# Weights loaded at once, magnitudes by one product with ones, and separate banks for row and column scores

## The chip, the core and the metric

The kernel runs on one core of a Trainium2 chip. A core has a matrix engine (TensorE: PE in the profile, its weight loads PEld), a vector engine (VectorE, DVE), a scalar engine (ScalarE, ACT), a general one (GpSimd, POOL), and a queue engine (SyncE, SP) that here issues all DMAs. Each engine runs its own instructions in the order of the program and waits on the others through semaphores. On-chip data lie in SBUF; TensorE writes into PSUM, eight banks of 128 x 512 float32, which VectorE and ScalarE read.

The metric is the time of one execution on the device in microseconds (us): the median of several runs.

## What is computed

Two kinds of layers alternate, four in all, each with a residual and a layer norm ahead (x is 2048 x 512):

```
def _A_ref(x, wq, wk, wv, wo, beta):          # 32 heads of 16, 4 segments of 512 rows
    q, k, v = x @ wq, x @ wk, x @ wv
    for s in range(4):
        p = softmax(qs @ ks.T * scale + causal mask);  a_dot = p @ vs
        a_mem = phi(qs) @ M / (phi(qs) @ z + 1e-6)
        o = g * a_mem + (1 - g) * a_dot                # g = sigmoid(beta)
        M += phi(ks).T @ vs;  z += sum of phi(ks)
    return o @ wo
def _B_ref(x, ...):                            # Fourier mixing, real part
    a, b = x @ dft_hid_re.T, x @ dft_hid_im.T
    return dft_seq_re @ a - dft_seq_im @ b
x = x + _A(norm(x));  x = x + _B(norm(x));  x = x + _A(norm(x));  x = x + _B(norm(x))
```

An attention layer with the Fourier layer behind it is called a layer below: there are two (0 and 1), with the same weights and the same Fourier matrices.

## The kernel before

**Numbers.** The products run on float16 pairs: each matrix is scaled by a power of two and split into a high and a low half, and three products (high-high, high-low, low-high) make one. To split a weight the kernel needs its largest magnitude. `absmax` (line 345) takes it for each partition, and `scales` (348) takes it over partitions: a transpose on TensorE, a maximum on VectorE, a diagonal (`dg`), a product with ones on TensorE, which hands the value to all partitions, and three small integer operations that make the scale and its inverse. `split` (367) then writes the high half on ScalarE and the low half on VectorE, which scales and subtracts in one operation.

**Work.** Each layer has 4 segments of 4 groups of 8 heads: groups 0 to 31 in all. A group passes these streams in turn:

- `s_p` (682) projects queries and keys, `s_v` (707) values. `t_split` (584) writes the halves of Q and K to DRAM and gathers them into `qst` and `kst`, which have two buffers each (`NR`); a group waits there for the column scores of the group two before it, and its values wait for the value products of that group.
- `s_x` (777) makes the row scores, in pairs of banks. `t_max` (766) takes their masked maxima on VectorE into `mx`. When a group's maxima are all there, TensorE transposes them, ScalarE and VectorE halve them (`mhl`), and four small DMAs put them into rows of `qst`.
- `s_st` (827) makes the column scores, in pairs of banks too, with the maxima taken off by those rows; `t_sel` (816) takes their exponentials on ScalarE and clears the masked part on GpSimd. `s_av` (849) multiplies them with the values, two accumulators a group, `s_m` (869) merges them with the memory part of `s_mem` (730).
- `s_o` (904) makes the output products with `wo` when four groups of a segment are merged and all weights are ready (`WO`); `t_res` adds the residual and normalizes. `s_ab` (1010) makes the Fourier products over the hidden dimension, `s_f` (1041) those over the sequence, two row tiles (at the end of a layer four) as a chunk. `s_r` (944) and `s_c` (962) load the sequence matrix in 128 pieces, scale and split them in batches of four and store them for layer 1; they begin when `WO` is done.

**Weights before.** At the start SP loads four tiles of x, then the query and key weights of group column 0 (256 KB each). `s_w` (376) goes group column by group column: magnitudes of its query and key weights, `scales`, `split` of both, a store of the split weight for later use. The other ten loads and `beta` are issued within the first column, when the four tiles of segment 0 are normalized and transposed. The value weights have one scale, which needs all four of them. `s_wo` (415) loads `wo` and `wd` into the same space `y` when it is free, and splits them in twelve steps.

**Order.** The program is one list of instructions that a planner writes at build time. Each stream yields what it needs next (an engine, tiles to read, slots to take) and the loop at the end (1080 on) asks `Plan.ready` when that could start by an estimate of all durations, and takes the stream that could start first. A pair of score banks is held back up to 1000 ns (`TWICE`) while other products are ready, unless two pairs are free. `Plan.setup` (72) makes pools of slots with a reserve and a cap for each kind: the eight PSUM banks (`pj` projections and other products, `av` value products, `dft` Fourier products, `ss` scores of both sorts) and 50 slots of SBUF. A kind may go over its reserve only when slots are left beyond the unmet reserves of the others. `weights` (665) fetches split weights ahead, as many as its kind may hold at that moment.

All engines' calls go through one helper, so nearly all instructions of the profile carry its line, 237; groups are told apart by tiles. `b` is any PSUM bank, `w` any SBUF slot, `g` the two slots of transposed rows.

Of the kernel before, what the change touches and what calls it, by code (L numbers as in the profile page):

```python
# [10 lines left out]
I32 = mybir.dt.int32  # L11
# [20 lines left out]
SLACK = 0  # L32
# [211 lines left out]
def body(ctx: ExitStack, tc: tile.TileContext, x, wq, wk, wv, wo, beta, wd, cs, out):  # L244
# [40 lines left out]
    load(0, 1)  # L285
    macc = const.tile([128, NG, 2, 4, 32], F32, name="macc")
# [34 lines left out]
    def spawn(g):  # L321
        tasks.append([next(g, None), g])
# [8 lines left out]
    mk = const.tile([128, 1], F32, name="mk")  # L331
    V.memset(mk, 0.0)
# [15 lines left out]
    def scales(a, b):  # L348
        k = b - a
        yield need("T", amax[:, b - 1:b], tag="ss")  # L350
        pm = ps("ss")
        T.transpose(pm[0:k, 0:128], amax[:, a:b], identf)
        yield need("V", pm)
        V.tensor_reduce(mk[0:k], pm[0:k, 0:128], axis=AX.X, op=OP.max)
        V.tensor_scalar(mk[0:k], mk[0:k], 1e-30, None, op0=OP.max)
        dg = rg("dg", 3, F32, (128, 4))
        V.tensor_scalar(dg[:, 0:k], identf[:, 0:k], mk, None, op0=OP.mult)
        yield need("T", dg)
        T.matmul(pm[:, 256:256 + k], ones, dg[:, 0:k], start=True, stop=True)
        yield need("V", pm)  # L360
        gi, si, vi = (t[:, a:b].bitcast(I32) for t in (gmax, scl, inv))
        V.tensor_scalar(gi, pm[:, 256:256 + k].bitcast(I32), 0x7F800000, None, op0=OP.bitwise_and)
        pl.close(pm)
        V.tensor_scalar(si, gi, -1.0, float(268 << 23), op0=OP.mult, op1=OP.add)
        V.tensor_scalar(vi, gi, 1.0, -float(14 << 23), op0=OP.mult, op1=OP.add)
# [6 lines left out]

    def flat(t):
        return t.rearrange("p a b -> p (a b)")

    def s_w():
        def part(n, g):
# [3 lines left out]
            yield from split(w, stage[g][n], scl[:, i:i + 1])  # L381
# [5 lines left out]
        for g in range(NG):  # L387
# [3 lines left out]
            yield from scales(2 * g, 2 * g + 2)  # L391
            for f, n, e in ((f_q, 0, -10), (f_k, 1, -10), (f_k2, 1, 12)):
                V.tensor_scalar(f[g], inv[:, 2 * g + n:2 * g + n + 1], 2.0 ** e, None, op0=OP.mult)
            V.tensor_scalar(f_s[g], inv[:, 2 * g:2 * g + 1], inv[:, 2 * g + 1:2 * g + 2], 2.0 ** 22,
                            op0=OP.mult, op1=OP.mult)
            yield from part(0, g)
            yield from part(1, g)
            if g == 0:
                yield gate(*[("L", 0, t) for t in range(TT)])
                Y.dma_start(gb[:, 0, :], beta)  # L400
                for j in range(NG):
                    load(j, 2)
                    if j:
                        load(j, 0)
                        load(j, 1)
                for j in range(NG):
                    yield need("V", stage[j][2])
                    V.tensor_reduce(vm[:, j:j + 1], flat(stage[j][2]), axis=AX.X, op=OP.max,
                                    apply_absolute_value=True)
                V.tensor_reduce(amax[:, 8:9], vm, axis=AX.X, op=OP.max)  # L410
                yield from scales(8, 9)
                done.add("WL")
            yield from part(2, g)

    def s_wo():
        wos = y[:, 12:16, :]
        yield gate("WL")
        Y.dma_start(wos, wo.rearrange("(t p) n -> p t n", p=128))
        yield gate(("W", 0, 3), ("W", 1, 3))
        wds = y[:, 0:8, :].rearrange("p (t e) n -> p t (e n)", e=2)  # L420
        Y.dma_start(wds, wd.rearrange("(t p) n -> p t n", p=128))
        pm = const.tile([128, 12], F32, name="pmax")
        for i in (12, 13, 14, 15, *range(8)):
            yield need("V", y[:, i, :])
            V.tensor_reduce(pm[:, (i + 4) % 16:(i + 4) % 16 + 1], y[:, i, :], axis=AX.X, op=OP.max,
                            apply_absolute_value=True)
        yield need("V", pm)
        for i, sl in ((9, slice(0, 4)), (10, slice(4, 12))):
            V.tensor_reduce(amax[:, i:i + 1], pm[:, sl], axis=AX.X, op=OP.max)
            yield from scales(i, i + 1)  # L430
        yield need("V", scl[:, 10:])
        V.tensor_scalar(sneg, scl[:, 10:], -1.0, None, op0=OP.mult)
        V.tensor_scalar(f_o, inv[:, 8:9], inv[:, 9:10], 2.0 ** 9, op0=OP.mult, op1=OP.mult)
        V.tensor_scalar(f_y, inv[:, 10:11], 2.0 ** 9, None, op0=OP.mult)
        for k in range(KT):
            yield from split(w_o[:, :, k], wos[:, k], scl[:, 9:10])
        for e, s in enumerate((scl[:, 10:], sneg)):
            for k in range(KT):
                yield from split(w_d[:, :, k, 512 * e:512 * e + 512], wds[:, k, 512 * e:512 * e + 512], s)
        done.add("WO")  # L440
# [324 lines left out]

    def t_max(sp, mx, a, p0, w, t, left):
# [10 lines left out]
    def s_x():  # L777
        for i in range(NGRP):
# [3 lines left out]
            left = [0]  # L782
            for t in range(TT):
# [14 lines left out]
            yield need("T", mx, tag="ss")  # L798
            pm = ps("ss")
# [27 lines left out]
    def s_st():  # L827
        for i in range(NGRP):
            yield gate(("X", i))
            qs, ks = qst[i % NR], kst[i % NR]  # L830
            for t in range(TT):
                n = 512 - 128 * t
                w = 512 // n
                for p0 in range(0, NP, w):
                    yield need("T", qs, ks, tag=("ss", "ss", "pt", "pt"), mode="h")
                    sp = [ps("ss"), ps("ss")]
# [234 lines left out]
    streams = [[None, s()] for s in (s_r, s_c, s_m, s_av, s_st, s_o, s_ln, s_w, s_x, s_mem, s_v, s_p, s_ab, s_f, s_wo, s_k)]  # L1071
# [7 lines left out]
    while streams or tasks:  # L1079
# [24 lines left out]
        if pl.mode != "h":  # L1104
            other = min((r for r, s in ready if s[0][0] == "T" and s[0][3] != "h"), default=1e18)
            for j, (r, s) in enumerate(ready):
                w = s[0]
                if w[2][:2] == ("ss", "ss") and r + EARLY >= other:
                    both = pl.ready(w[1], w[2] + ("ss", "ss"), w[0])
                    late = raw[id(s)] + TWICE  # L1110
                    ready[j] = max(r, late if both is None else min(both, late)), s
        if ready:
            first = min(r for r, _ in ready)
            best = next(q for q in ready if q[0] <= first + SLACK)
# [49 lines left out]
```

## Time and profile before

| | us |
|---|---|
| runs: lowest, median, highest of 3 | 1827.49, 1828.71, 1836.32 |
| profiled execution: span from first to last instruction | 1824.8 |
| TensorE busy | 1697.8 (93%) |
| VectorE busy | 1085.9 (60%) |
| ScalarE busy | 897.1 (49%) |
| GpSimd busy | 724.6 (40%) |
| mean granted TensorE clock | 0.971 |

No time is listed for the profiled execution other than its span; the median of the runs is 3.9 us above that span. In the page's 40 slices a digit is the busy share of a slice (45.6 us) in tenths, and the clock is in tenths of full speed:

```profile
PE   3878799989989999999999879999999999999999
DVE  7786955577765877565556655564656567533211
PEclk8988899999999999999999898999999999999999
```

In a row of the timeline stand start, length, engine, operation, written tile, read tiles, count, and in brackets the idle time before it with what ended it. In a row of groups stand count, busy time in all, mean ns of one, and the idle time of the engine just before them with what ended it. A row of waits gives engine, what it waited for, us in all, times, longest.

### The profile page before, as it was taken

How to read it: one execution, taken by the hardware profiler on the slowest of the kernel's cores; microseconds unless marked ns; L12 is line 12 of the kernel's file. 1: busy time of each engine (PE TensorE's matmuls, PEld its weight loads, DVE VectorE, ACT ScalarE, POOL GpSimd, SP SyncE). 2: the span in 40 equal slices, each digit the busy share in tenths (PEclk: the TensorE clock that was granted, in tenths of full speed). 3: DMA queues.
4: the chain of work that ended last, by engine and by line, in shares of the span. 5: the costliest groups of instructions: out<-in, count | busy, mean ns of one | idle time of the engine just before them, and what ended most of it. 6: DMA issues, size and time to landing. Idle time of an engine off the chain costs nothing. (4 is left out here: it accounts for less than half of the span.)

```text
span 1824.8 us, 32643 instructions
## 1 busy us (share of the span) xinstructions
PE 1697.8 (93%) x11045; PEld 742.2 (41%) x11045; DVE 1085.9 (60%) x3404; ACT 897.1 (49%) x1563; POOL 724.6 (40%) x1158
## 2 busy tenths in 40 slices
PE   3878799989989999999999879999999999999999
PEld 2433334443433434344444333434444434444444
DVE  7786955577765877565556655564656567533211
ACT  2557656757465666644436655555445444431000
POOL 3234545546363464553434543442534334231000
PEclk8988899999999999999999898999999999999999
DMA  7345535655454653345784541553544444222233
GB/s 190 105 135 132 170 74 165 156 152 150 127 147 136 191 149 102 119 151 167 232 226 156 136 124 49 144 131 100 132 110 114 141 120 102 83 84 81 93 122 115
DMA packets 240985, 242.44 MB, mean 133 GB/s; under 512 B 129777, under 2 KB 152305, under 8 KB 240817
## 3 DMA queue, kind: packets, MB, share of 16 engines
q1 hardware_dynamic: 240816, 240.35, 46.9%
q8 instruction: 87, 1.43, 0.3%
q14 instruction: 82, 0.66, 0.1%
HBM read 152.96 MB, written 63.70 MB: 119 GB/s over the span
## 5 line engine op out<-in xcount | busy, mean ns | idle before, releaser
L237 PEld LDWEIGHTS <-w 128*128 128x128 f16 x4992 | 463.8, 98 | 613.3 <-issue 113.0
L237 PE MATMUL b<-w,w 128*128 128x512 f16 x3072 | 708.9, 380 | 2.0 <-ACT w L237 1.7
L237 POOL TENSOR_TENSOR w<-w,w 128x512 f16<-128x512 f32 (+1 forms) x316 | 380.6, 1208 | 412.6 <-ACT w L237 266.9
L237 ACT ACTIVATE w<-b,fac 128x512 f32<-128x512 f32 (+1 forms) x728 | 420.9, 658 | 176.6 <-PE b L237 156.0
L237 DVE CUSTOM_DVE_ANT_0 junk<-b,cmask 128x128 bf16<-128x128 f32 (+3 forms) x1024 | 437.6, 485 | 77.7 <-PE b L237 76.3
L237 POOL TENSOR_SCALAR_AFFINE_SELECT w<-w 128x128 f32<-128x128 f32 (+2 forms) x704 | 242.4, 357 | 309.5 <-ACT w L237 302.6
L237 DVE SCALAR_TENSOR_TENSOR y<-b,fyu,y 128x512 f32<-128x512 f32 x200 | 149.2, 746 | 217.7 <-PE b L237 217.2
L237 ACT ACTIVATE w<-b 128x512 f32<-128x512 f32 (+1 forms) x240 | 138.2, 600 | 251.9 <-PE b L237 240.4
L237 ACT ACTIVATE w<-w,csc 128x512 f16<-128x512 f32 (+1 forms) x256 | 181.1, 721 | 60.7 <-DVE csc L237 51.5
L237 PE MATMUL b<-g,w 128*128 128x512 f16 x768 | 190.4, 391 | 7.4 <-DMA g<-w 5.8
L237 PE MATMUL b<-w,vt 128*32 128x512 f32 (+3 forms) x2048 | 186.2, 460 | 3.0 <-POOL w L237 2.2
L237 PE MATMUL b<-wd,w 128*128 128x512 f16 x768 | 178.7, 380 | 0.9 <-DVE w L237 0.5
L237 ACT ACTIVATE w<-w 128x512 f16<-128x512 f32 (+1 forms) x144 | 90.7, 635 | 168.5 <-DVE w L237 117.4
L237 DVE SCALAR_TENSOR_TENSOR w<-b,w 128x512 f16<-128x512 f32 x128 | 88.1, 688 | 132.6 <-ACT w L237 131.9
L237 PE MATMUL b<-kst,qst 62*128 62x128 f16 (+3 forms) x1024 | 131.9, 314 | 25.3 <-DMA kst<-d 10.0
L237 PE MATMUL b<-qst,kst 64*128 64x512 f16 (+3 forms) x1024 | 123.8, 308 | 16.4 <-ACT w L237 6.1
L237 PE MATMUL b<-w,g 128*128 128x128 f16 x1536 | 99.5, 224 | 10.9 <-DVE mx L237 4.8
L237 PEld LDWEIGHTS <-g 128*128 128x128 f16 x1536 | 91.2, 100 | 25.1 <-issue 14.5
L237 PEld LDWEIGHTS b<-w,vt 128*32 128x32 f32 x2048 | 55.9, 111 | 101.0 <-issue 56.4
L237 PEld LDWEIGHTS <-kst 64*128 64x128 f16 x1024 | 38.3, 95 | 137.2 <-issue 124.7
L237 PE MATMUL b<-wo,w 128*128 128x512 f16 x384 | 89.7, 379 | 0.2 <-ACT w L237 0.2
L237 DVE DVE_READ_ACCUMULATOR2_ANT mx<- 128x1 f32 x1024 | 84.5, 83 | 0.0
(102 smaller groups left out, 887.1 us busy)
## 6 DMA issues: line engine op xcount, KB each, us to landing
w<-in_cs_dram SPq DMA_DIRECT2D x128, 256.0 KB
cc<-w SPq DMA_DIRECT2D x128, 256.0 KB
w<-cc SPq DMA_DIRECT2D x128, 256.0 KB
w<-w SPq DMA_DIRECT2D x96, 256.0 KB
d<-w SPq DMA_DIRECT2D x128, 128.0 KB
w<-rec SPq DMA_DIRECT2D x56, 256.0 KB
w<-in_x_dram SPq DMA_DIRECT2D x32, 256.0 KB
qst<-d SPq DMA_DIRECT2D x64, 128.0 KB
```

The source lines that it names most:

```text
L237: r = f(*args, **kw)
```

## The change

- All twelve loads of the query, key and value weights and `beta` are issued at the start, behind the four tiles of x.
- `scales` takes one product of ones with the magnitudes of the partitions: a sum over partitions in place of the maximum, handed to all of them. It takes a bank of the kind `dft`. Query and key weights of column 0 have a call of their own; the other seven magnitudes share one.
- A new helper `share` splits all weights but the first two: ScalarE writes the high half and scales the source in place, and GpSimd or VectorE (whichever `tt` picks) subtracts. `split` stays for the first two.
- The slots for split weights may go up to 8 (`wt`) and 4 (`wv`), from 3 and 2.
- Row scores take banks of the kind `sx`, column scores of the kind `st`, each with a reserve of two and a cap of four, until the output products of segment 0 are let through; then `together` sets the shares of before, and groups that begin after that take `ss` again. A group keeps the kind that it began with.
- The rule that holds a pair of score banks back now applies to any request that begins with a score bank, the single one for the transposed maxima included.
- The loop's choice among streams has a rank as second key; `RANK` is empty, so that all have the same.

```diff
+APART = dict(pj=(1, 4), av=(1, 2), dft=(0, 2), sx=(2, 4), st=(2, 4), ss=(0, 4))
+SHARED = dict(pj=(1, 4), av=(2, 2), dft=(1, 2), sx=(0, 2), st=(0, 2), ss=(2, 4))
...
-    pl.setup(psum, "b", 8, dict(pj=(1, 4), av=(2, 2), dft=(1, 2), ss=(2, 4)))
+    pl.setup(psum, "b", 8, dict(APART))
...
-        en=(1, 1), wt=(2, 3), wv=(1, 2), craw=(4, 8), cc=(4, 8), pt=(8, 12), ot=(4, 8), xb=(2, 4),
+        en=(1, 1), wt=(2, 8), wv=(1, 4), craw=(4, 8), cc=(4, 8), pt=(8, 12), ot=(4, 8), xb=(2, 4),
...
     load(0, 0)
     load(0, 1)
+    Y.dma_start(gb[:, 0, :], beta)
+    for j in range(NG):
+        for n in range(3):
+            if j or n == 2:
+                load(j, n)
...
     def scales(a, b):
         k = b - a
-        yield need("T", amax[:, b - 1:b], tag="ss")
-        pm = ps("ss")
-        T.transpose(pm[0:k, 0:128], amax[:, a:b], identf)
-        yield need("V", pm)
-        V.tensor_reduce(mk[0:k], pm[0:k, 0:128], axis=AX.X, op=OP.max)
-        V.tensor_scalar(mk[0:k], mk[0:k], 1e-30, None, op0=OP.max)
-        dg = rg("dg", 3, F32, (128, 4))
-        V.tensor_scalar(dg[:, 0:k], identf[:, 0:k], mk, None, op0=OP.mult)
-        yield need("T", dg)
-        T.matmul(pm[:, 256:256 + k], ones, dg[:, 0:k], start=True, stop=True)
-        yield need("V", pm)
+        yield need("T", amax[:, b - 1:b], tag="dft")
+        pm = ps("dft")
+        T.matmul(pm[:, :k], ones, amax[:, a:b], start=True, stop=True)
+        yield need("V", pm)
+        V.tensor_scalar(gmax[:, a:b], pm[:, :k], 1e-30, None, op0=OP.max)
...
+    def share(o, src, s):
+        yield need("A", src, s)
+        A.activation(o[:, 0], src, AF.Copy, scale=s)
+        A.activation(src, src, AF.Copy, scale=s)
+        yield need("VG", o, src)
+        tt(o[:, 1], src, o[:, 0], OP.subtract)
...
+        for n in range(2):
+            yield need("V", stage[0][n])
+            absmax(n, flat(stage[0][n]))
+        yield from scales(0, 2)
+        yield from part(0, 0, split)
+        yield from part(1, 0, split)
+        for j in range(1, NG):
             for n in range(2):
-                yield need("V", stage[g][n])
-                absmax(2 * g + n, flat(stage[g][n]))
...
+                yield need("V", stage[j][n])
+                absmax(2 * j + n, flat(stage[j][n]))
+        for j in range(NG):
+            yield need("V", stage[j][2])
+            V.tensor_reduce(vm[:, j:j + 1], flat(stage[j][2]), axis=AX.X, op=OP.max,
+                            apply_absolute_value=True)
+        V.tensor_reduce(amax[:, 8:9], vm, axis=AX.X, op=OP.max)
+        yield from scales(2, 9)
+        factors(0, NG)
+        done.add("WL")
+        yield from part(2, 0, share)
+        for g in range(1, NG):
+            for n in range(3):
+                yield from part(n, g, share)
...
         for k in range(KT):
-            yield from split(w_o[:, :, k], wos[:, k], scl[:, 9:10])
+            yield from share(w_o[:, :, k], wos[:, k], scl[:, 9:10])
...
+    apart = [True]
+    kinds = pl.area["ss"]["kinds"]
+
+    def scores(which):
+        return "s" + which if apart[0] else "ss"
+
+    def together():
+        apart[0] = False
+        kinds.update(SHARED)
...
-                    yield need("T", qs, ks, tag=("ss", "ss"), mode="h")
-                    sp = [ps("ss"), ps("ss")]
+                    yield need("T", qs, ks, tag=(kx, kx), mode="h")
+                    sp = [ps(kx), ps(kx)]
...
             yield gate(("M", q * NG + NG - 1), "WO")
+            if not q:
+                together()
...
-                if w[2][:2] == ("ss", "ss") and r + EARLY >= other:
-                    both = pl.ready(w[1], w[2] + ("ss", "ss"), w[0])
+                if w[2][:1] in (("ss",), ("sx",), ("st",)) and r + EARLY >= other:
+                    both = pl.ready(w[1], w[2] + w[2][:2], w[0])
```

More of the change, by code (lines that the diff above doesn't have):

```diff
@@ L376, in s_w, with part @@
     def s_w():
-        def part(n, g):
+        def part(n, g, how):
             i = 2 * g + n if n < 2 else 8
@@ L380, in part @@
             w = sb("wv" if n == 2 else "wt", F16, (128, 2, KT, 128))
-            yield from split(w, stage[g][n], scl[:, i:i + 1])
+            yield from how(w, stage[g][n], scl[:, i:i + 1])
             yield need("Y", w)
@@ L385, in part @@
             done.add(("W", n, g))
-        for g in range(NG):
-            for n in range(2):
-                yield need("V", stage[g][n])
-                absmax(2 * g + n, flat(stage[g][n]))
[L391 to L413, printed above, removed]
@@ new lines, in factors @@
+        def factors(a, b):
+            for f, n, e in ((f_q, 0, -10), (f_k, 1, -10), (f_k2, 1, 12)):
+                for g in range(a, b):
+                    V.tensor_scalar(f[g], inv[:, 2 * g + n:2 * g + n + 1], 2.0 ** e, None, op0=OP.mult)
+            for g in range(a, b):
+                V.tensor_scalar(f_s[g], inv[:, 2 * g:2 * g + 1], inv[:, 2 * g + 1:2 * g + 2], 2.0 ** 22,
+                                op0=OP.mult, op1=OP.mult)
+        for n in range(2):
+            yield need("V", stage[0][n])
+            absmax(n, flat(stage[0][n]))
@@ L435, in s_wo @@
         for k in range(KT):
[L436 removed]
+            yield from share(w_o[:, :, k], wos[:, k], scl[:, 9:10])
         for e, s in enumerate((scl[:, 10:], sneg)):
             for k in range(KT):
[L439 removed]
+                yield from share(w_d[:, :, k, 512 * e:512 * e + 512], wds[:, k, 512 * e:512 * e + 512], s)
         done.add("WO")
@@ L782, in s_x @@
             left = [0]
+            kx = scores("x")
             for t in range(TT):
@@ L830, in s_st @@
             qs, ks = qst[i % NR], kst[i % NR]
+            kt = scores("t")
             for t in range(TT):
@@ L1112, in body @@
         if ready:
-            first = min(r for r, _ in ready)
-            best = next(q for q in ready if q[0] <= first + SLACK)
+            best = min(ready, key=lambda q: (q[0], q[1][2]))
         if best is None:
```

21 lines of the change are left out of this document (10 added, 11 removed).

## The prediction

> **What bounds the kernel now.** I read the page's busy shares and slices first, then the busy times by stretch, then TensorE's waits and the vector engine's groups inside the stretch that stood out. Columns of the stretches: length, then busy time and count of PE, PEld, DVE, ACT, POOL, then granted clock, DMA share, GB/s.
>
> ```profile
> 0.00:40.00 40.00, 12.09 (x49) 6.00 (x50) 29.47 (x85) 8.30 (x14) 15.15 (x22) 0.89 0.79 207
> 40.00:240.00 200.00, 164.54 (x1196) 71.06 (x1194) 156.20 (x570) 117.99 (x210) 78.17 (x148) 0.87 0.45 129
> 240.00:1000.00 760.00, 732.02 (x4732) 326.51 (x4733) 488.67 (x1456) 444.40 (x749) 366.77 (x515) 0.99 0.54 154
> 1000.00:1100.00 100.00, 82.05 (x648) 34.37 (x647) 62.63 (x248) 57.20 (x105) 42.19 (x86) 0.88 0.49 128
> 1100.00:1824.80 724.80, 707.12 (x4425) 304.30 (x4423) 348.90 (x1049) 269.25 (x486) 222.27 (x388) 0.99 0.39 108
> ```
>
> TensorE bounds nearly all of it. From 240 to 1000 us it is busy 732.0 of 760 (96%) at clock 0.99, from 1100 to the end 707.1 of 724.8. Of the 127 us that it sits idle (each row's length less its PE), 27.9 lie before 40 us, 35.5 between 40 and 240, 18.0 at the change of layer. From 40 to 240 the granted clock is also only 0.87: 13% of 164.5 busy us, 21 us, are slow clock. So that stretch loses about 57 us, and what is gained there reaches the end, because behind it TensorE has work without a break. What fills TensorE later, the output products and the Fourier products, can't start before the four groups of segment 0 are through; the first output product runs at 229.8:
>
> ```profile
> L237 PE MATMUL b<-wo,w x60: 376/379/390, 229.8 to 420.0; 128*128 128x512 f16 x60
> ```
>
> How fast do the groups go through? The row maxima of a group end in four small stores into `qst`; these are the first four groups (start, length):
>
> ```profile
> 57.91 2.51 SPq L237 DMA_DIRECT2D qst<-mhl  x4
> 97.71 2.48 SPq L237 DMA_DIRECT2D qst<-mhl  x4
> 129.44 2.76 SPq L237 DMA_DIRECT2D qst<-mhl  x4
> 168.99 2.50 SPq L237 DMA_DIRECT2D qst<-mhl  x4
> ```
>
> One group takes 39.8, 31.7, 39.6 us. VectorE's groups between 40 and 240 us (busy, mean ns, then its idle time) say what of this is work:
>
> ```profile
> L237 DVE CUSTOM_DVE_ANT_0 junk<-b,cmask 128x128 bf16<-128x128 f32 (+3 forms) x192 | 81.2, 485 | 6.9 <-PE b L237 6.6
> L237 DVE DVE_READ_ACCUMULATOR2_ANT mx<- 128x1 f32 x191 | 15.7, 82 | 0.0
> L237 DVE SCALAR_TENSOR_TENSOR w<-y,scl,w 128x512 f16<-128x512 f32 x9 | 6.6, 735 | 0.3 <-ACT w L237 0.3
> L237 DVE TENSOR_REDUCE cam<-w 128x1 f32<-128x512 f32 x8 | 4.9, 674 | 0.0
> L237 DVE SCALAR_TENSOR_TENSOR wd<-y,sneg,wd 128x512 f16<-128x512 f32 x4 | 3.9, 967 | 1.0 <-ACT wd L237 1.0
> L237 DVE SCALAR_TENSOR_TENSOR wd<-y,scl,wd 128x512 f16<-128x512 f32 x4 | 3.8, 966 | 0.6 <-ACT wd L237 0.6
> L237 DVE TENSOR_REDUCE amax<-y 128x1 f32<-128x512 f32 x5 | 3.2, 673 | 0.0
> L237 DVE SCALAR_TENSOR_TENSOR wo<-y,scl,wo 128x512 f16<-128x512 f32 x4 | 3.0, 762 | 0.0
> L237 DVE TENSOR_REDUCE mk<-b 2x1 f32<-2x128 f32 (+1 forms) x5 | 1.4, 275 | 2.0 <-PE b L237 2.0
> L237 DVE TENSOR_SCALAR dg<-identf,mk 128x2 f32<-128x2 f32 (+1 forms) x5 | 1.1, 223 | 0.2
> ```
>
> 192 maxima are six groups, so a group's maxima cost (81.2 + 15.7) / 6 = 16.2 us, under half of its period. VectorE is the busiest helper (78% of the stretch), and TensorE's first wait there is on it:
>
> ```profile
> PE b L237 <- DVE mx L237: 13.6, 15, 3.9
> PE b L237 <- ACT w L237: 6.3, 14, 1.3
> PE b L237 <- DVE dg L237: 2.2, 1, 2.2
> ```
>
> Why the second group is late, a look at the order of time shows: its weights are late.
>
> ```profile
> 38.20 19.61 SPq L237 DMA_DIRECT2D w<-w  x3
> 55.67 0.75 DVE L237 SCALAR_TENSOR_TENSOR w<-y,scl,w 128x512 f16<-128x512 f32 x1
> 71.35 1.71 SPq L237 DMA_DIRECT2D kst<-d  x4
> 60.00:80.00 20.00, 19.91 (x177) 9.74 (x176) 9.00 (x25) 17.10 (x31) 8.17 (x22) 1.00 0.55 149
> 80.00:100.00 20.00, 16.54 (x128) 8.38 (x128) 19.45 (x91) 6.31 (x12) 3.25 (x4) 0.74 0.30 80
> ```
>
> The split of group 1's weights stands behind all maxima of group 0 (to 55.67), its projections can only follow, its keys are gathered at 71.35, and its maxima run after that. From 60 to 80 us VectorE, the busiest helper, is busy 9.0 of 20 us, for want of maxima, while TensorE is full with projections that it could have made before; from 80 to 100 VectorE is full (19.5) and TensorE waits and slows down (16.5 at clock 0.74). The two take turns where they could run side by side.
>
> **The change part by part.**
>
> *Loads.* Ten 256 KB loads and `beta` move from behind the first transposes to 3.6 us. Their issues fit ahead of the first transpose, but not their bytes.
>
> ```profile
> 3.13 0.51 SPq L237 DMA_DIRECT2D y<-in_wk_dram  x1
> 9.35 7.59 SPq L237 DMA_TRANSPOSE g<-w  x4
> 4.00:6.00 2.00, 0.00 (x0) 0.00 (x0) 1.86 (x7) 0.00 (x0) 0.70 (x2) 1.00 1.02 306
> 12.00:14.00 2.00, 0.59 (x2) 0.50 (x2) 1.84 (x7) 0.18 (x1) 0.05 (x1) 1.00 1.01 193
> 18.87 8.23 PE L237 MATMUL b<-g,w 128*128 128x512 f16 x24 [5.79 <-DMA g<-w]
> 30.41 0.27 PE L237 MATMUL b<-identf,amax 128*1 128x128 f32 x1 [3.31 <-DVE amax L237]
> 36.54 0.27 PE L237 MATMUL b<-w,g 128*128 128x128 f16 x1 [4.02 <-ACT w L237]
> ```
>
> SP needs 10 x 0.51 + 0.45 us and is free near 9.3, when the first transpose is ready. But 16 tiles of 262 KB at 306 GB/s take 13.7 us: from 2 to about 15.7. Transposes ran at 193 GB/s, 1.36 us a tile. Served after the weights they end at 15.7 + 5.4 = 21.1, and with the 1.9 us from the last issue (9.35 + 7.59 = 16.94) to the product, the first product starts at 23.0 instead of 18.87: 4 us lost. Served at once, nothing is lost. Against it: the loads no longer hold SP and the DMA engines at 19 to 27 us, where the first stores of Q and K stood behind them, and the V weights' scale no longer waits for loads at 30.41 and 36.54 (3.3 + 4.0 us). New is that V waits for the magnitudes of all weights: ten reductions of 0.67 us on VectorE in place of four, 4 us; behind that wait stand only ACT's and POOL's halves of V, which the second group of products needs later than Q and K. Bounds for the first 40 us: 4 lost, 7 gained; I take 0, as the two largest rows nearly cancel. [...]
>
> *Magnitudes by one product.* A call of `scales` loses a transpose, a reduction (275 ns), `dg` (223) and a round to TensorE; the clamp stays. There are four calls instead of seven. In the stretch from 40, five become two: 5 x (0.275 + 0.223) = 2.5 us for the two operations lost, and 3 x 3 small integer ones, priced like `dg` (0.223), for the calls that fall away, 2.0: -4.5 us of VectorE. The sum over partitions in place of the maximum costs nothing in time.
>
> *Subtractions moved.* Nine weight splits, 6.6 us, and twelve of `wo` and `wd`, 10.7 us, leave VectorE; five magnitudes (3.2) move ahead of 40 us. With the calls that is 25 us off VectorE's 156. They land on ACT and POOL:
>
> ```profile
> L237 ACT ACTIVATE w<-y,scl x12: 704/708/821, 14.4 to 97.7; 128x512 f16<-128x512 f32 x12
> L237 POOL TENSOR_TENSOR w<-w,w 128x512 f32<-128x512 f32 (+1 forms) x30 | 36.9, 1237 | 30.6 <-ACT w L237 23.3 <-DMA w<-rec 5.8 <-DVE w L237 1.4
> ```
>
> 22 more activations of 0.71 are 15.6 us of ACT, 22 subtractions of 1.24 are 27 of POOL; ACT was 59%, POOL 39% busy from 40 to 240, so both have room. The price without that room: SP's stores of split weights wait for POOL, and what stands behind them on SP (gathers of `qst` and `kst`) waits too; at most the 19.6 us that SP stood at 38.20. [...]
>
> *Weights early, `wt` to 8.* All splits can be done by about 45 us, so that the projections of groups 1 to 3 no longer stand behind maxima. What is late next: `qst` has two buffers, so group i+2's gather waits for group i's column scores; and VectorE's maxima themselves.
>
> *Banks apart.* Until the first output products, row scores (`sx`) and column scores (`st`) each keep two banks and may take four, where both shared four. Column scores of group i run beside row scores of i+1. The projections keep at least one bank, as before, usually two.
>
> *Sum for 40 to 240.* Lower end: only the VectorE waits named above shrink, half of 13.6 plus 2.2, 9 us, less 3 for order: -6. Upper end: TensorE's own 143 us (164.5 less 21.4) at the 96% of the next stretch take 149: -51. Between: VectorE at its present 78% does 131 us in 168: -32. I take that, since VectorE's row is the nearest, less what comes forward: `wo` and `wd` done earlier lets the sequence matrix be prepared before the output products, some 12 pieces of 0.67 us, 8 us of VectorE, 10 us at 78%. -32 + 10 = -22.
>
> *After 240.* At the first output products the banks are joined again, as before. Two edits stay: weights may hold more slots (rival below), and the rule that holds a pair of scores back up to 1 us now holds the transpose of the maxima too, 32 times. Its bounds are 32 us lost, if each lay on the chain of the end, and the 18.0 us idle at the change of layer gained, if it let other products pass there. I take 0: the next groups' products fill TensorE, 96% busy. The change of layer keeps its 18 us.
>
> Total: span 1824.8 - 22 = 1803. The profiled execution has no time listed beside its span; the median of the runs, 1828.7, stands 3.9 above it. Predicted **1807 us**.
>
> **The rivals.**
>
> 1. *The start takes it back, or the banks do nothing.* Transposes at 23 us (+4), groups still in turn because `qst` or the exponentials of ACT hold them, and only VectorE's named waits shrink (-6): 1827, no change. For it: ACT is already in TensorE's waits (6.3 us). Against it: VectorE's empty time after 57 us. 22%.
>
> 2. *Slots, slower.* The work pool has 50 slots; the kinds' reserves add to 45, five are loose. Before, `wt` and `wv` could take two of them beyond their reserve; now all five, and they fetch ahead as soon as a slot is free. In the tail of layer 0, when the groups are done and layer 1's weights sit waiting, raw and prepared pieces of the sequence matrix then have four slots each. Fourteen batches of four pieces lie between these products (the first six with one output column per piece, eight with two):
>
> ```profile
> 756.43 0.39 PE L237 MATMUL b<-cam,ones 128*128 128x4 f32 x2 [2.22 <-DVE cam L237]
> 987.71 0.61 PE L237 MATMUL b<-cam,ones 128*128 128x2 f32 x4
> PE b L237 <- DVE cam L237: 9.9, 10, 2.3
> ```
>
> If only the last piece of a batch shows, that is one activation and one subtraction, 0.71 + 1.24 = 1.95 us; if all of its chain shows, a reduction (0.67), the product (0.39), six small operations (1.2), two activations and a subtraction, 4.9. Fourteen times that is 27 to 69; between them, 48: 1855. It decides when the loose slots are held by weights there and no other product is ready. For it: TensorE waits for `cam` already. Against it: four prepared pieces cover some 11 us of products. 15%.
>
> 3. *All of the room taken.* The groups follow each other at VectorE's speed and the clock stays up: -40, 1789. 13%.
>
> **How the numbers follow.** Forecast (1797 to 1819, all faster) 50%, rival 1 22%, rival 2 15%, rival 3 13%. A measurement of this kernel tells about 0.5%, 9 us, from no change. Faster: 50 + 13 = 63%; within: 22%; slower: 15%. The range leaves out rival 2 but its low end, and the far end of rival 3: 1784 to 1835.
>
> **What would show it.** Right: the four stores of row maxima of group 1 near 78 instead of 97.7, of group 3 before 150 instead of 169; the first output product near 190 instead of 229.8; clock from 40 to 240 above 0.92; no weight subtraction on VectorE after the first two. Wrong: first product after 23, SP standing long at weight stores, or TensorE's waits on `cam` and on C pieces between 740 and 1000 grown above 10 us.

## The result

| | before | changed |
|---|---|---|
| median of 4 runs, us | 1828.10 | 1799.56 |
| lowest and highest, us | 1825.83 to 1836.32 | 1795.83 to 1800.83 |
| profiled execution: span, us | 1824.8 | 1799.1 |
| TensorE idle in the span, us | 127.0 | 106.4 |
| mean granted clock | 0.971 | 0.972 |

The ratio is 0.9831, with a 95% interval of 0.9807 to 0.9854: 28.5 us, or 1.7%, faster. The profiled execution of the changed kernel took 1800.83 us, 1.7 more than its span. The helper's line is 239 now.

Busy times by stretch of the changed kernel, in the cuts of the prediction (length; busy time and count of PE, PEld, DVE, ACT, POOL; clock; DMA share; GB/s):

```profile
0.00:40.00 40.00, 16.12 (x97) 8.51 (x98) 27.27 (x76) 12.81 (x20) 16.66 (x22) 1.00 0.83 210
40.00:240.00 200.00, 165.15 (x1209) 70.24 (x1207) 143.97 (x537) 134.57 (x237) 103.22 (x178) 0.86 0.48 130
240.00:1000.00 760.00, 741.92 (x4870) 330.55 (x4869) 490.61 (x1493) 454.09 (x768) 375.70 (x533) 1.00 0.56 160
1000.00:1100.00 100.00, 81.93 (x565) 32.59 (x566) 63.65 (x244) 55.40 (x101) 44.96 (x89) 0.80 0.38 93
1100.00:1799.10 699.10, 687.52 (x4300) 298.12 (x4298) 334.81 (x1004) 255.95 (x461) 210.29 (x362) 1.00 0.40 110
```

The row from 40 to 240 is a surprise: TensorE is idle for 34.9 us there (35.5 before) at clock 0.86 (0.87 before). By the clock on the wall that stretch loses as much as it did. The idle time went elsewhere: 4.0 us less before 40, 9.9 less from 240 to 1000, 6.1 less from 1100 on. So a cut at fixed times can't say what a stretch gained, because another mix of work runs in it. Marks of the work say more. The stores of the row maxima, of groups 0 to 3, and the first output product:

```profile
64.14 3.71 SPq L239 DMA_DIRECT2D qst<-mhl  x4
84.22 2.40 SPq L239 DMA_DIRECT2D qst<-mhl  x4
115.68 2.51 SPq L239 DMA_DIRECT2D qst<-mhl  x4
138.42 2.44 SPq L239 DMA_DIRECT2D qst<-mhl  x4
L239 PE MATMUL b<-wo,w x58: 377/379/390, 207.3 to 419.8; 128*128 128x512 f16 x58
```

Group 0 is 6 us later than before, group 1 is 13.5 earlier, group 2 13.8, group 3 30.6, the first output product 22.5. (At group 3 the stores gain more than the maxima ahead of them: the transpose of its maxima is 26.2 us earlier, at 136.0 instead of 162.2.) Then the lead stays as it is: the first store of layer 0's result goes out at 850.7 instead of 873.1, 22.4 earlier. From there to the end of the span it is 948.4 us instead of 951.7. So of the 25.7 us between the two spans, 22.4 are there at the first store of layer 0's result, as at the first output product, and 3.3 come behind it.

### The profile page after: what moved, and what is told of

It is laid out like the page before. It is cut to its first block, busy times and chain, and to the rows that moved or that the text cites. A ratio compares the mean times of both kernels' runs of the same rounds, so it can differ in the third digit from the quotient of the medians.

```text
span 1799.1 us, 32616 instructions
## 1 busy us (share of the span) xinstructions
PE 1692.7 (94%) x11032; PEld 740.0 (41%) x11032; DVE 1060.3 (59%) x3352; ACT 912.8 (51%) x1585; POOL 750.8 (42%) x1183
## 5 line engine op out<-in xcount | busy, mean ns | idle before, releaser
L239 ACT ACTIVATE w<-b 128x512 f32<-128x512 f32 (+1 forms) x240 | 138.4, 599 | 243.3 <-PE b L239 235.5
L239 ACT ACTIVATE w<-w 128x512 f16<-128x512 f32 (+1 forms) x144 | 90.4, 632 | 171.9 <-DVE w L239 124.9
L239 PE MATMUL b<-kst,qst 62*128 62x128 f16 (+3 forms) x1024 | 136.4, 315 | 17.3 <-DVE mx L239 10.6
L239 PE MATMUL b<-qst,kst 64*128 64x512 f16 (+3 forms) x1024 | 127.5, 311 | 19.5 <-DVE mx L239 8.8
L239 PEld LDWEIGHTS b<-w,vt 128*32 128x32 f32 x2048 | 59.0, 112 | 100.0 <-issue 55.8
L239 DVE DVE_READ_ACCUMULATOR2_ANT mx<- 128x1 f32 x1024 | 84.7, 83 | 0.0
```

Of the source, the lines that this page charges most:

```text
L239: r = f(*args, **kw)
```

## The experiments

Theory A: segment 0 goes faster because weights are early and VectorE has less to do. Rival B: the separate banks are the source. Rival C: the list is a planner's, and any new order moves the time by as much. Twelve kernels, each an edit of the changed kernel or of the one before. Every edit also makes the planner write a new list, so each run shows its edit together with a new order. All marks are of the profiled executions, in us: "mx 1" and "mx 3" are the starts of the transposes of the maxima of groups 1 and 3, "out" is the first output product, "y" the first store of layer 0's result.

| kernel | median | ratio to before, 95% interval | mx 1 | mx 3 | out | y | out to y |
|---|---|---|---|---|---|---|---|
| before | 1828.1 | | 96.5 | 162.2 | 229.8 | 873.1 | 643.3 |
| changed | 1799.6 | 0.9831 [0.9807, 0.9854] | 82.9 | 136.0 | 207.3 | 850.7 | 643.4 |
| join | 1833.9 | 1.0014 [0.999, 1.0038] | 95.1 | 158.0 | 224.4 | 883.5 | 659.2 |
| banks_only | 1841.3 | 1.007 [1.0046, 1.0094] | 97.6 | 154.7 | 231.3 | 887.6 | 656.3 |
| hold720 | 1799.7 | 0.9832 [0.9812, 0.9851] | 84.3 | 137.2 | 211.1 | 853.5 | 642.4 |
| switch97 | 1816.7 | 0.993 [0.9906, 0.9954] | 83.6 | 136.8 | 207.2 | 866.9 | 659.7 |
| split_all | 1823.2 | 0.994 [0.992, 0.9961] | 85.9 | 137.9 | 214.2 | 868.6 | 654.5 |
| late_loads | 1823.2 | 0.9943 [0.9921, 0.9966] | 94.6 | 152.3 | 227.2 | 875.5 | 648.3 |
| few_slots | 1817.0 | 0.9918 [0.9892, 0.9945] | 82.3 | 135.4 | 208.8 | 863.0 | 654.2 |
| pairs_only | 1802.2 | 0.9834 [0.9806, 0.9861] | 81.5 | 134.4 | 206.7 | 849.4 | 642.7 |
| before_switch97 | 1835.5 | 1.0031 [1.001, 1.0051] | 96.9 | 171.9 | 237.0 | 872.0 | 635.1 |
| before_hold720 | 1828.6 | 0.9981 [0.9959, 1.0004] | 97.9 | 166.0 | 232.8 | 876.8 | 644.0 |
| old_scales | 1830.0 | 0.9991 [0.9973, 1.0009] | 90.9 | 145.6 | 229.6 | 883.2 | 653.6 |
| six_early | 1816.6 | 0.9912 [0.9878, 0.9946] | 87.2 | 138.5 | 217.7 | 861.9 | 644.2 |

The three groups of runs had medians of before of 1828.68, 1833.9 and 1830.32, so ratios, not medians, are to be compared across them.

**The banks: join and banks_only.** The first takes the separate banks out of the changed kernel:

```diff
-    pl.setup(psum, "b", 8, dict(APART))
+    pl.setup(psum, "b", 8, dict(SHARED))
...
-    apart = [True]
+    apart = [False]
```

> The changed kernel, but row and column scores share four banks from the start, as before; all else as changed. Theory A (early weights and the work taken off VectorE bring segment 0 forward, the banks add little): 1800 to 1808, first output product by 215 us. Theory B (the banks are the source): 1818 to 1828, first output product back near 228. Theory C (any new order of the list moves the time as much): anything from 1790 to 1830, and the two runs with a planner constant moved by 2 to 3% scatter as widely.

The second puts them, and the hold-back rule for pairs of all three kinds, into the kernel before; there `scales` takes a bank of the kind `dft`:

```diff
...
-        yield need("T", amax[:, b - 1:b], tag="ss")
-        pm = ps("ss")
+        yield need("T", amax[:, b - 1:b], tag="dft")
+        pm = ps("dft")
...
-                    yield need("T", qs, ks, tag=("ss", "ss"), mode="h")
-                    sp = [ps("ss"), ps("ss")]
+                    yield need("T", qs, ks, tag=(kx, kx), mode="h")
+                    sp = [ps(kx), ps(kx)]
...
```

> The kernel before with one part of the change alone: banks apart until the first output products (the magnitudes' bank is of the kind dft, since ss has no reserve then; loads, splits, slots and the hold-back rule for pairs as before). Theory A: 1822 to 1830, because group 1's weights are still late and the maxima of group 1 can't start before about 74 us. Theory B: 1800 to 1810. Theory C: anything.

Without the banks the whole gain is gone, so theory A's numbers for `join` were missed (1834 for 1800 to 1808, 224.4 for 215). Of the 34 us that `join` is slower than the changed kernel, 17 are there at the first output product; the 16 behind it are as many as order alone moves there (below). With the banks alone nothing is gained either: 1841, slower than before, outside theory A's 1822 to 1830 too, and rival B's number was missed by more. Neither part does it alone. TensorE's order of time shows why; the rows here and below are picked out. In the changed kernel, group 1's row scores (`b<-kst,qst`) start at once behind group 0's transposed maxima, and from 71 us they run between group 0's column scores (`b<-qst,kst`):

```profile
61.24 0.28 PE L239 MATMUL b<-identf,mx 128*32 128x128 f32 x1 [0.77 <-DVE mx L239]
61.46 0.83 PE L239 MATMUL b<-kst,qst 62*128 62x128 f16 x16
71.15 1.42 PE L239 MATMUL b<-qst,kst 64*128 64x512 f16 x4 [4.17 <-DVE mx L239]
72.51 0.50 PE L239 MATMUL b<-kst,qst 62*128 62x384 f16 x2
72.78 0.89 PE L239 MATMUL b<-qst,kst 64*128 64x512 f16 x2
82.90 0.28 PE L239 MATMUL b<-identf,mx 128*32 128x128 f32 x1 [0.48 <-DVE mx L239]
```

In `join` they start as early, but once the column scores come, one pair more gets through, at 73.44 us, and the rest run only behind the column scores, which end at 84.7. The edit takes nothing away but the banks of their own:

```profile
60.99 0.83 PE L239 MATMUL b<-kst,qst 62*128 62x128 f16 x16
70.92 2.99 PE L239 MATMUL b<-qst,kst 64*128 64x512 f16 x10 [4.40 <-DMA qst<-mhl]
73.44 1.05 PE L239 MATMUL b<-kst,qst 62*128 62x384 f16 x2
84.30 0.40 PE L239 MATMUL b<-qst,kst 64*128 64x128 f16 x8
86.03 0.34 PE L239 MATMUL b<-kst,qst 62*128 62x384 f16 x2
95.11 0.28 PE L239 MATMUL b<-identf,mx 128*32 128x128 f32 x1 [0.30 <-DVE mx L239]
```

In `banks_only` the banks are free, but group 1's keys are not there: they are gathered at 71.44 us, as late as before (71.35), and not at 50.14 as in the changed kernel. Its row scores begin at 78.25. First `banks_only`, then the changed kernel:

```profile
71.44 1.72 SPq L239 DMA_DIRECT2D kst<-d  x4
```

```profile
50.14 2.21 SPq L239 DMA_DIRECT2D kst<-d  x4
```

**The loads: late_loads.** The ten loads go back behind the first transposes; column 0's factors are then made at once.

```diff
-    Y.dma_start(gb[:, 0, :], beta)
-    for j in range(NG):
-        for n in range(3):
-            if j or n == 2:
-                load(j, n)
...
+        factors(0, 1)
         yield from part(0, 0, split)
         yield from part(1, 0, split)
+        yield gate(*[("L", 0, t) for t in range(TT)])
+        Y.dma_start(gb[:, 0, :], beta)
+        for j in range(NG):
+            for n in range(3):
+                if j or n == 2:
+                    load(j, n)
...
-        factors(0, NG)
+        factors(1, NG)
```

> The changed kernel, but the ten loads and beta are issued when the first four tiles are transposed, as before (column 0's factors are then made at once, since its projections come before the other loads). First projection back near 18.9 from 22.5 us. Theory A: the weights of groups 1 to 3 come some 5 us later, the start 4 us earlier: first output product 204 to 212. Theory B: the same, 203 to 209. A rival that early loads are the source: 220 or later.

The rival's number came, 227, and theory A's was missed. The first projection is back at 18.2 us, but group 1's keys are late: its row scores begin at 69.5, waiting for its data, 8 us later than in the changed kernel, and its maxima are transposed at 94.6 instead of 82.9:

```profile
57.19 0.40 SPq L239 DMA_DIRECT2D y<-in_wd_dram  x1
58.11 2.74 SPq L239 DMA_DIRECT2D kst<-d  x4
69.00 0.69 DVE L239 TENSOR_REDUCE pmax<-y 128x1 f32<-128x512 f32 x1 [3.24 <-DMA y<-in_wd_dram]
69.50 0.21 PE L239 MATMUL b<-kst,qst 62*128 62x128 f16 x1 [1.38 <-DMA d<-w]
```

Late weights alone don't explain the 8 us. The gathers of the keys are issued at 58.11 us, 8 us later than in the changed kernel but still ahead of group 0's maxima (61.27). They were issued right behind the load of `wd`, 2 MB, and the first reader of `wd` and the first reader of the keys both wait until 69.0 to 69.5 us. In the changed kernel that load goes out behind the gathers, at 59.20. So this run doesn't part late weights from a large load that the new order put ahead of the keys.

By `join` and `banks_only`, free banks and early keys are both needed for group 1's maxima to follow group 0's, and the early loads serve the second. Taking away the banks or the early loads costs 17 and 20 of the 22.5 us at the first output product.

**The subtractions: split_all.** `share` calls `split`, so that 22 subtractions are VectorE's again.

```diff
     def share(o, src, s):
-        yield need("A", src, s)
-        A.activation(o[:, 0], src, AF.Copy, scale=s)
-        A.activation(src, src, AF.Copy, scale=s)
-        yield need("VG", o, src)
-        tt(o[:, 1], src, o[:, 0], OP.subtract)
+        yield from split(o, src, s)
```

> The changed kernel, but with the old split for all weights: the 22 subtractions go back to VectorE. The first runs showed that two things must be told apart: the time of the first output product (207 us in the changed kernel, 230 before, 224 with joined banks, and within 4 us of 207 when only a planner constant moves), and the stretch from there to the first store of layer 0's result (643 us before and changed, 643 to 660 otherwise). Theory A (work off VectorE matters beside the banks): first output product 5 to 15 us later, 212 to 222. Theory B (banks alone): 205 to 211. The whole time follows with 10 us of scatter from the second stretch.

Theory A's number: 214.2, 6.9 us later, where a new order alone moved this mark by up to 3.7 (`hold720`). Groups 1 and 3 come 3.0 and 1.9 us later than in the changed kernel; the other 5 us lie behind them. The edit also takes 22 activations off ScalarE, so the 7 us are what remains of both.

**The magnitudes: old_scales.** `scales` takes the transpose, the maximum, the diagonal and the second product again, in a bank of the kind `dft`.

```diff
...
-        T.matmul(pm[:, :k], ones, amax[:, a:b], start=True, stop=True)
-        yield need("V", pm)
-        V.tensor_scalar(gmax[:, a:b], pm[:, :k], 1e-30, None, op0=OP.max)
+        T.transpose(pm[0:k, 0:128], amax[:, a:b], identf)
+        yield need("V", pm)
+        V.tensor_reduce(mk[0:k], pm[0:k, 0:128], axis=AX.X, op=OP.max)
+        V.tensor_scalar(mk[0:k], mk[0:k], 1e-30, None, op0=OP.max)
+        dg = rg("dg", 3, F32, (128, 8))
+        V.tensor_scalar(dg[:, 0:k], identf[:, 0:k], mk, None, op0=OP.mult)
+        yield need("T", dg)
+        T.matmul(pm[:, 256:256 + k], ones, dg[:, 0:k], start=True, stop=True)
+        yield need("V", pm)
+        V.tensor_scalar(gmax[:, a:b], pm[:, 256:256 + k], 1e-30, None, op0=OP.max)
```

> The changed kernel, but the magnitudes are taken over partitions as before (transpose, maximum, diagonal, second product; bank of the kind dft). Theory A prices it at 2 us of VectorE and a round to TensorE in each of four calls: first output product 207 to 212. If this part carries the gain: 218 or later.

This part, priced at a few us, takes all of the gain with it; theory A's 207 to 212 was missed by 18. In its trace the scale of the seven later magnitudes is made 5 us later (VectorE in order of time, first the changed kernel, then this one):

```profile
29.45 0.17 DVE L239 TENSOR_SCALAR scl<-gmax 128x7 int32<-128x7 int32 x1
```

```profile
29.22 1.27 DVE L239 TENSOR_REDUCE vm<-y 128x1 f32<-128x512 f32 x2
34.42 0.17 DVE L239 TENSOR_SCALAR scl<-gmax 128x7 int32<-128x7 int32 x1
```

The added operations of VectorE are below 1 us (0.27, 0.14 and 0.23). The planner put other work between: two of the four `vm` reductions, a memset, and the split of a projection. From there everything slides: the maxima of group 0 are transposed at 67.4 instead of 61.2, of group 3 at 145.6 instead of 136.0, and the output products come at 229.6. So this kernel has early weights and free banks, and its maxima come earlier than before the change, by 5.6 us in group 1 and 16.6 in group 3; yet its first output product is where it was. From group 3's maxima to that product it takes 84 us, where the changed kernel takes 71 and the one before 68. What holds it there, the late scale or another order of the list, this run can't tell.

**Slots and the hold-back rule: few_slots and pairs_only.**

```diff
-        en=(1, 1), wt=(2, 8), wv=(1, 4), craw=(4, 8),
+        en=(1, 1), wt=(2, 3), wv=(1, 2), craw=(4, 8),
```

> The changed kernel, but split weights may hold 3 and 2 slots as before. Theory A: the split of later groups' weights waits for slots again, first output product 215 to 230. Theory B: 205 to 211. The slot rival of the prediction (weights take loose slots from the sequence matrix): the stretch from the first output product to the first store of layer 0's result becomes shorter than 643, 625 to 638.

```diff
-                if w[2][:1] in (("ss",), ("sx",), ("st",)) and r + EARLY >= other:
+                if w[2][:2] in (("ss", "ss"), ("sx", "sx"), ("st", "st")) and r + EARLY >= other:
```

> The changed kernel, but the hold-back rule applies to pairs of banks alone, so that the transpose of the maxima isn't held. Theories A and B: first output product 204 to 211, the whole within 10 us of 1799.6 either way. A rival that this rule is the source of the gain: over 1815, with waits of TensorE on mx back above 36 us.

Neither matters for segment 0: 208.8 and 206.7, so theory A's 215 to 230 for `few_slots` was missed. The slot rival of the prediction wanted a shorter stretch from output product to `y` with few slots; it got a longer one, 654. The hold-back of the single bank makes no difference that can be measured.

**What order alone does: four kernels with a planner's constant moved.** HOLD 720 for 700, or SWITCH 97 for 95 ns, in the changed kernel and in the one before. No work differs.

> The changed kernel with one constant of the planner moved, HOLD 720 instead of 700 ns: no work differs, only the order in places. Theory A and B: within 5 us of 1799.6. Theory C: off by 10 us or more in either direction.

> The changed kernel with another constant of the planner moved, SWITCH 97 instead of 95 ns: no work differs. Theory A and B: within 5 us of 1799.6. Theory C: off by 10 us or more.

> The kernel before with the planner constant HOLD 720 instead of 700 ns: no work differs. As for the other: first output product within 4 us of 229.8 either way; the whole 1822 to 1850 if order scatters, within 5 us of 1828 if not.

> The kernel before with the planner constant SWITCH 97 instead of 95 ns: no work differs. If a new order alone moves the stretch from the first output product to the first store of layer 0's result by up to 16 us, as it did in the changed kernel, the whole lies between 1822 and 1850, with the first output product still within 4 us of 229.8. If before's order is steady: within 5 us of 1828.

The two kernels' first output products stay apart: 207, 211, 207 against 230, 233, 237. But the stretch behind them moves: 643, 642, 660 against 643, 644, 635. A 2 ns constant cost the changed kernel 17 us, all of it between the first output product and `y`. So rival C's number came for `switch97` and theory A's for `hold720`; and the first output product of `before_switch97`, 7 us late, is outside the 4 us that were expected. Rival C holds for the stretch behind the first output product and not for that product. The rows from 240 to 1000 us of the changed kernel and of `switch97` differ by 10 us of idle TensorE and a little clock:

```profile
240.00:1000.00 760.00, 731.49 (x4688) 323.75 (x4687) 482.42 (x1461) 441.15 (x746) 367.68 (x514) 0.99 0.55 156
```

It is spread. TensorE's waits from 205 to 860 us, two rows of the changed kernel, then the same two of `switch97` (us in all, times, longest):

```profile
PE b L239 <- DVE cam L239: 1.3, 1, 1.3
PE b L239 <- ACT w L239: 0.7, 2, 0.6
```

```profile
PE b L239 <- ACT w L239: 7.1, 12, 2.5
PE b L239 <- DVE cam L239: 5.1, 5, 1.7
```

No single wait carries the 16 us, and no run here isolates their cause.

**A version with a cheaper start: six_early.** Six loads early, four behind the transposes, magnitudes in three calls.

```diff
...
+    load(1, 0)
+    load(1, 1)
     for j in range(NG):
-        for n in range(3):
-            if j or n == 2:
-                load(j, n)
+        load(j, 2)
...
+        yield from scales(8, 9)
+        yield from scales(2, 4)
+        factors(1, 2)
+        yield gate(*[("L", 0, t) for t in range(TT)])
+        for j in range(2, NG):
+            load(j, 0)
+            load(j, 1)
...
```

> The changed kernel, but only six of the ten loads are early (query and key weights of group column 1, and all value weights); columns 2 and 3 are loaded when the first four tiles are transposed, and the magnitudes go in three calls, so that no weight of groups 0 and 1 waits for columns 2 and 3. If the late first projection (22.5 us) is the DMA queue behind ten loads, four loads of 0.83 us less bring it to 19 to 20; group 1's weights are as early, so the first output product comes at 200 to 208. Whole time: 1790 to 1799 with the shorter second stretch (643), 1803 to 1815 with the longer (657).

The first projection does come at 19.2 us, and group 0's maxima 0.9 us earlier, but group 1's come 4 us later and the first output product 10 us later. So 217.7 misses the 200 to 208 that were expected, and 1816.6 the whole time. The early start didn't carry over to the later groups. None of the twelve beats the changed kernel.

## Why the prediction was right, and where not

- **The total.** Predicted 1807 in 1784 to 1835, faster by 22; measured 1799.6, faster by 28.5. The stretch up to the first output product gave 22.5 of it. That the 22 meets the 22.5 so closely is luck, as the next points show: the place was right, the terms of the sum were not.
- **Where it is gained.** "What is gained there reaches the end, because behind it TensorE has work without a break": right, by marks (22.5 us at the first output product, 22.4 at `y`, 25.7 at the end). Wrong by the table that I argued from: 40 to 240 us was to lose less, with a clock above 0.92. It lost as much, at 0.86; the gain shows as less idle time behind it. Of the marks that were named, group 3's stores before 150 us came (138.4), group 1's near 78 came at 84.2, and the output product near 190 at 207.3.
- **The term for 40 to 240.** The sum took VectorE's load, 131 us at 78%, as the measure: -32. VectorE was busy 144 there, at 72%. The subtractions are off it (the two left are those of column 0), yet undoing that costs only 7 of the 22.5 us. The +10 for pieces of the sequence matrix that come forward wasn't seen: eight are reduced in this stretch, as many as before. And the lower end let TensorE's waits on the maxima shrink by half from 13.6 us; they grew to 21.9.

```profile
L239 DVE TENSOR_REDUCE cam<-w 128x1 f32<-128x512 f32 x8 | 5.2, 676 | 1.4 <-DMA w<-in_cs_dram 1.4
PE b L239 <- DVE mx L239: 21.9, 21, 5.0
```

  What moved segment 0 is not VectorE's load but the time at which group 1's maxima may start. Early keys and free banks both stand ahead of that start; the banks had no term of their own in the sum, and rival 1 spoke of the banks doing nothing. Banks or early loads undone alone cost 17 and 20 us, so their parts don't add. They aren't enough either: with the old magnitudes both are there, and the output product comes at 229.6.
- **"What is late next: `qst` ... and VectorE's maxima themselves."** From 140 to 160 us VectorE is nearly without work, and ACT is full:

```profile
120.00:140.00 20.00, 16.92 (x77) 4.47 (x80) 18.05 (x64) 18.28 (x33) 16.04 (x31) 0.59 0.32 78
140.00:160.00 20.00, 15.91 (x101) 5.40 (x93) 3.05 (x5) 17.15 (x31) 11.76 (x22) 0.90 0.61 180
```

  The exponentials of segment 0 and the doubled activations of `wo` and `wd` meet there. Group 3's maxima came 26 us earlier, the output products only 22.5, and were forecast near 190: by the rows this is where the rest may have gone. It stays argued, and one run speaks against the activations: `split_all` has 22 fewer, and from group 3's maxima to the first output product it takes 76 us, not less than the 71 of the changed kernel. Over all these kernels that way takes 65 to 84 us, and no run shows what sets it.
- **The loads.** With the transposes served after the weights the first projection was forecast at 23.0 us, and it came at 22.50, with 11.15 us of waiting for the transposes:

```profile
12.78 5.72 SPq L239 DMA_TRANSPOSE g<-w  x3
19.21 1.28 SPq L239 DMA_TRANSPOSE g<-w  x1
12.00:14.00 2.00, 0.00 (x0) 0.00 (x0) 1.88 (x7) 0.80 (x2) 0.26 (x1) 1.00 1.21 290
22.50 6.15 PE L239 MATMUL b<-g,w 128*128 128x512 f16 x15 [11.15 <-DMA g<-w]
```

  The way there was another, so the closeness is partly luck. SP was free of the loads at 12.7 us, where 9.3 was forecast from 0.51 us an issue: its issues took 1.63 us once and then 0.65 to 0.83. The first transpose was thus issued 3.4 us later than before, at 12.78, and the issue of the last ended 3.6 later, at 20.49. From there to the first product it is 2.0 us, 1.9 before. So nearly all of the 3.6 us stand in SP's own rows, where the forecast had SP free and the transposes waiting for the weights' bytes. The DMA engines do still carry 290 GB/s when the transposes are issued, and in `late_loads` gathers issued at 58.11 us, right behind a load of 2 MB, were waited for until 69.5 us; but here a wait behind the loads' bytes can't be told from SP's late issue. The first product comes at 18.2 us with no loads ahead, 19.2 with six, 22.5 with ten. In the sum I took 0 for the first 40 us; TensorE did 16.1 us of work there at full clock instead of 12.1 at 0.89, about 5 us gained, within the bounds. By the mark of group 0's maxima the start lost 5.4 us (61.2 instead of 55.8).
- **Magnitudes at 4.5 us of VectorE.** As work they are small, as priced: the old form adds 0.64 us to a call. As a place in the list they were mis-sized: putting the old form back costs 22 us at the first output product, in a list that begins to differ by 5 us at the scale of the seven later magnitudes.
- **Rival 2, the slots.** Not seen: TensorE's waits on `cam` in the whole span fell from 9.9 to 3.4 us, and fewer slots (`few_slots`) didn't shorten the stretch to `y`.

```profile
PE b L239 <- DVE cam L239: 3.4, 4, 1.3
```

- **The chances.** "Within 0.5%" and "slower" were given 37% for mechanisms of the change. The runs show another source that I didn't price: the order of a planned list, which moved one and the same work from 1799.6 to 1816.7. Three orders of the changed kernel have ratios of 0.983, 0.983 and 0.993, three of the one before 1, 0.998 and 1.003: means of 0.986 and 1.000. By that the change is worth some 25 us, and its own order is a good one; three orders each are few.

## What to carry to other kernels

When a chain of stages starts late, look for all conditions on its start: here the change without its banks kept 5 us at the first output product, without its early loads 3, and whole it gave 22. In a kernel whose order a planner writes, judge an edit by marks of the work that it should move, and move a constant that changes no work to see how far order alone goes, before a difference of 1% is put down to a mechanism. The busiest helper need not be the bound: VectorE was 78% busy, and giving the subtractions back to it cost 7 us of the 22.

## What was not expected of the hardware

Some of VectorE's operations with SBUF alone as source are longer in the changed kernel. The same kinds from 40 to 240 us, before and then changed:

```profile
L237 DVE TENSOR_SCALAR w<-w,mv,rs 128x512 f32<-128x512 f32 x4 | 3.0, 748 | 1.0 <-POOL rs L237 0.9
L237 DVE TENSOR_SCALAR w<-w,fac 128x512 f32<-128x512 f32 x6 | 2.9, 486 | 5.5 <-ACT w L237 5.2
```

```profile
L239 DVE TENSOR_SCALAR w<-w,mv,rs 128x512 f32<-128x512 f32 x4 | 4.0, 1012 | 0.2 <-POOL rs L239 0.2
L239 DVE TENSOR_SCALAR w<-w,fac 128x512 f32<-128x512 f32 x5 | 3.5, 708 | 4.0 <-ACT w L239 3.9
```

That is 4 x 0.26 + 5 x 0.22 = 2.2 us, an eighth of the 17.3 us of subtractions (6.6 and 10.7) that left VectorE. The order of time shows which ones are long. A pair of the changed kernel, then one of the kernel before; the last row is an operation of the changed kernel that starts with no GpSimd operation on two sources under way:

```profile
51.40 1.16 POOL L239 TENSOR_TENSOR w<-y,w 128x512 f16<-128x512 f32 x1 [0.69 <-ACT y L239]
51.96 0.87 DVE L239 TENSOR_SCALAR w<-w,fac 128x512 f32<-128x512 f32 x1 [0.24 <-ACT w L239]
143.32 1.15 POOL L237 TENSOR_TENSOR w<-w,w 128x512 f16<-128x512 f32 x1
143.38 1.37 DVE L237 TENSOR_SCALAR w<-w,mv,rs 128x512 f32<-128x512 f32 x1 [0.93 <-POOL rs L237]
107.71 0.49 DVE L239 TENSOR_SCALAR w<-w,fac 128x512 f32<-128x512 f32 x1 [0.65 <-ACT w L239]
```

In these two kernels, from 40 to 240 us, an operation of these kinds that starts while GpSimd works on two sources from SBUF ends 0.27 to 0.29 us behind GpSimd's, however early it started. Six of the nine in the changed kernel are such, and one of the ten before. In `old_scales` it went the other way once: GpSimd's took 1.61 us beside one of 0.53. Only three of the six stand behind moved subtractions. In `late_loads` and `old_scales`, where GpSimd has the subtractions too, the means are 693 and 510, and 737 and 538 ns. So how often it happens is a matter of order, and the 2.2 us are not a price of the move as such. No run shows what ties the two ends together. The maxima kept their 485 ns (192 of them in this stretch, before and changed).
